# Moving one output matmul from ahead of the second score burst of each batch to behind it, in a fused attention and GEGLU kernel

## The chip, the cores and the metric

The kernel runs on one core of one Trainium2 chip. The metric is device time in microseconds of one execution. A profile of a single execution belongs to each kernel; its span is some 1.8 to 2 us shorter than the metric, as it runs from the first to the last instruction of the program.

## The reference

Eight batches of causal attention (8 heads, 576 positions, 16 "beacon" keys that every query sees, head size 64) are followed by a feed-forward block with a gated GELU on all 4608 rows.

```python
scores = scale * q @ k_all.T            # k_all: beacon keys, then the batch's own
scores = where(causal, -1e9, scores)
a = exp(scores - max);  a /= a.sum()
x = a @ v_all                           # then heads side by side: 4608 x 512
out = (gelu(x @ w_gate) * (x @ w_val)) @ w_out
```

## The kernel before

For each batch b, TensorE carries two jobs in one program order: attention of batch b, and the output product of the feed-forward block of batch b - 1. `o(n)` issues the next n of 48 output matmuls (128x128 by 128x512). `scores(b, ...)` makes one score tile with half-height matmuls (two heads side by side in the array), and lets ScalarE exponentiate it; GpSimd then masks the diagonal. `av_head` and `av` are the products of weights and values, which VectorE normalizes. The output matmuls are there to fill TensorE's time while ScalarE exponentiates.

```python
psum_s = tile_pool(name="psum_s", bufs=3, space=PSUM)    # score tiles
psum_t = tile_pool(name="psum_t", bufs=1, space=PSUM)
psum_o = tile_pool(name="psum_o", bufs=1, space=PSUM)
# ...
def scores(b, *parts):
    s_ps = psum_s.tile([P, 2, 512], FP32, name="s_ps", tag="s")
    # ... matmuls of each part into s_ps
    act(exp_ring[...], s_ps[...], ACT.Exp, scale=QK_SCALE)
    # ... GpSimd's masks
# in the loop over batches, b >= 1; on the right the names that this text uses
# (calls of ahead(2), which issue loads for later batches, are left out)
    o(3)
    scores(b, (0, 0)); scores(b, (0, 2)); scores(b, (0, 1))           # A1 A2 A3
    o(5)
    if b == 1: transpose_pe(1, 3)
    o(5)
    scores(b, (0, 3), (1, 3)); scores(b, (1, 0)); scores(b, (1, 2))   # B1 B2 B3
    o(5)
    av_head(b, 0, 0, psum_t, "t")
    o(1)
    scores(b, (1, 1)); scores(b, (2, 0)); scores(b, (2, 2))           # C1 C2 C3
    av_head(b, 0, 1, psum_t, "t"); turn_dma(b, 0)
    o(7)
    scores(b, (2, 1)); scores(b, (2, 3), (3, 3)); scores(b, (3, 0))   # D1 D2 D3
    av_head(b, 1, 0, psum_o, "o")
    o(5)
    av_head(b, 1, 1, psum_o, "o"); turn_dma(b, 1)
    scores(b, (3, 1)); scores(b, (3, 2))                              # E1 E2
    av(b, 2); turn_dma(b, 2)
    o(6)
    av(b, 3); turn_dma(b, 3)
    o(11)
    # ... then the gate and value matmuls of batch b
```

Score tiles take turns in three buffers (`bufs=3`), so a tile can be written only when the exponential that reads the tile three places before it has ended.

The softmax here doesn't subtract the row's maximum and nothing guards it: scores larger than these inputs give would overflow.

## Time and profile before

| | before |
|---|---|
| time, median of 3 runs | 366.03 us (366.0 to 366.04); the profiled execution took 366.35 us |
| span of the profile | 364.4 us |
| TensorE busy, share of the span | 97% |
| ScalarE, VectorE, GpSimd busy | 52%, 43%, 44% |
| from batch to batch, first score matmul to first score matmul, batches 2 to 7 | 38.877 us (mean of 5) |

The busy share of TensorE can't tell a stream without holes from one with small ones: the matmul records overlap (one lasts 379 ns, but the next starts 216 ns later), so a hole of 100 ns between two starts doesn't show as idle time. One has to compare starts with starts. The last row of the table does that for a whole batch; it repeats within 3 ns.

### The profile page before, as it was taken

To read this page: it belongs to the slowest core of one execution; us is meant where nothing else is said; L and a number is where in the kernel's file an instruction comes from. 1 tells how busy PE (TensorE), PEld (TensorE's weight loads), DVE (VectorE), ACT (ScalarE), POOL (GpSimd) and SP (SyncE) were. 2 spreads that over 40 slices of the span, in tenths; PEclk is the share of its full clock that TensorE was granted. 3 is DMA by queue.
4 is the path that set the end of the run, shared out by engine and by line. 5 is a ranking of instruction groups with operands and counts; after the bars stand their busy time and mean duration, and the time that the engine had idled before them with its cause. 6 is when DMAs were issued, how large, how long until landed. Compare 5 with 4: busy or idle time off the path is not lost.

```text
span 364.4 us, 7627 instructions
## 1 busy us (share of the span) xinstructions
PE 354.3 (97%) x3127; PEld 184.6 (51%) x3170; DVE 155.4 (43%) x305; ACT 189.0 (52%) x243; POOL 161.2 (44%) x288
## 2 busy tenths in 40 slices
PE   7899999999999999999999999999999999999996
PEld 6664446444654456445644464446544564444443
DVE  4546545433454335343533354434444353333332
ACT  3973489136933594339723892379335953321210
POOL 8934388565537452954475554646330530000000
PEclk9999999999999999999999999999999999999999
DMA  7999999799069995999299927991697033000103
GB/s 103 175 203 204 197 124 91 125 187 186 20 121 126 199 87 65 171 216 64 57 146 208 126 35 120 178 197 24 108 142 132 17 64 114 0 0 31 58 34 112
DMA packets 160419, 41.57 MB, mean 114 GB/s; under 512 B 146944, under 2 KB 155904, under 8 KB 160384
## 3 DMA queue, kind: packets, MB, share of 16 engines
q0 software_dynamic: 104848, 19.11, 69.5%
q1 hardware_dynamic: 55536, 21.96, 29.3%
q8 instruction: 25, 0.41, 0.5%
q14 instruction: 10, 0.08, 0.1%
HBM read 38.27 MB, written 9.44 MB: 131 GB/s over the span
## 4 chain that ended last, share of the span: by engine, by line
PE 94%; issue 1%; DMA 1%; DVE 1%; POOL 1%; POOLq 0%; DVEq 0%
PE gv_ps L168 48%; PE o_ps L168 25%; PE x_ps L168 9%; PE s_ps L168 8%; PE v_ps L168 2%; PE g_ps L168 2%; DMA qk<-in_q_dram 1%; PE t_ps L176 1%; DVE qkT L213 1%; POOL qk L111 0%; PE y_ps L176 0%; DVE hT_sb L426 0%; POOL eye L480 0%; DVE o_sb L445 0%; DVE qkT L217 0%
## 5 line engine op out<-in xcount | busy, mean ns | idle before, releaser
L171 ACT ACTIVATE ge_sb<-gv_ps 128x512 bf16<-128x512 f32 x101 | 59.4, 597 | 142.8 <-PE gv_ps L168 140.6
L426 DVE TENSOR_TENSOR hT_sb<-gv_ps,ge_sb 128x512 bf16<-128x512 f32 x101 | 69.0, 691 | 113.5 <-ACT ge_sb L171 111.1
L168 PE MATMUL gv_ps<-xT_sb,wg_sb 128*128 128x512 bf16 x402 | 111.4, 379 | 0.5
L168 PE MATMUL gv_ps<-xT_sb,wv_sb 128*128 128x512 bf16 x388 | 107.9, 379 | 0.4
L171 ACT ACTIVATE expT<-s_ps 128x992 bf16<-128x992 f32 (+3 forms) x112 | 100.6, 974 | 6.5 <-PE s_ps L168 5.4
L168 PE MATMUL o_ps<-wo_sb,hT_sb 128*128 128x512 bf16 (+2 forms) x420 | 99.9, 373 | 2.0 <-issue 0.9
L298 POOL TENSOR_SCALAR_AFFINE_SELECT expT<-expT 128x256 bf16<-128x256 bf16 (+1 forms) x140 | 52.3, 390 | 52.9 <-ACT expT L171 51.8
L168 PEld LDWEIGHTS <-wv_sb 128*128 128x128 bf16 x432 | 42.3, 98 | 50.6
L168 PEld LDWEIGHTS <-wg_sb 128*128 128x128 bf16 x432 | 42.0, 98 | 50.0
L168 PEld LDWEIGHTS <-hT_sb 128*128 128x128 bf16 x444 | 39.9, 98 | 41.7 <-issue 1.7
L168 PEld LDWEIGHTS <-expT 128*128 128x128 bf16 (+1 forms) x960 | 33.6, 97 | 9.8 <-DVE y_sb L334 2.9
L445 DVE COPY o_sb<-o_ps 128x512 f32<-128x512 f32 (+2 forms) x37 | 24.9, 672 | 31.2 <-PE o_ps L168 30.2
L168 PE MATMUL x_ps<-v_sb,expT 128*128 128x65 bf16 (+1 forms) x960 | 37.4, 193 | 0.0
L111 POOL DMA_DIRECT2D v_sb<-in_v_dram x40 | 33.6, 857 | 5.9 <-DMA wv_sb<-in_moe_w_val_dram 1.7
L168 PE MATMUL s_ps<-qkT 64*128 64x80 bf16 (+5 forms) x528 | 33.1, 250 | 2.3 <-DVE qkT L217 1.3
L111 POOL DMA_DIRECT2D k_sb<-in_k_dram x30 | 25.2, 842 | 14.7 <-DMA q_sb<-in_q_dram 11.3
L334 DVE TENSOR_TENSOR y_sb<-x_ps,r_sb 128x320 bf16<-128x320 f32 (+1 forms) x47 | 28.8, 612 | 1.6
L111 POOL DMA_DIRECT2D q_sb<-in_q_dram x30 | 25.3, 874 | 5.2 <-DMA wo_sb<-in_moe_w_out_dram 3.6
L332 DVE RECIPROCAL r_sb<-x_ps 128x5 f32<-128x5 f32 (+1 forms) x47 | 9.6, 204 | 42.3 <-PE x_ps L168 42.3
L168 PEld LDWEIGHTS <-qkT 64*128 64x128 bf16 x528 | 17.1, 95 | 17.8 <-issue 12.9
L377 POOL COPY hold_sb<-xT_sb 128x2 bf16<-128x2 bf16 x6 | 1.1, 186 | 31.1 <-DMA xT_sb<-y_sb 31.1
L111 POOL DMA_DIRECT2D k_sb<-in_beacon_k_dram x6 | 3.2, 534 | 13.4 <-DMA v_sb<-in_v_dram 13.4
(54 smaller groups left out, 123.3 us busy)
## 6 DMA issues: line engine op xcount, KB each, us to landing
out_dram<-o_sb SPq DMA_DIRECT2D x35, 256.0 KB, 7.0
v_sb<-in_v_dram POOLq DMA_DIRECT2D x24, 128.0 KB, 9.1
q_sb<-in_q_dram POOLq DMA_DIRECT2D x18, 128.0 KB, 11.8
k_sb<-in_k_dram POOLq DMA_DIRECT2D x18, 128.0 KB, 5.9
wo_sb<-in_moe_w_out_dram POOLq DMA_DIRECT2D x3, 512.0 KB, 14.4
wg_sb<-in_moe_w_gate_dram POOLq DMA_DIRECT2D x2, 512.0 KB, 11.4
wv_sb<-in_moe_w_val_dram POOLq DMA_DIRECT2D x2, 512.0 KB, 13.0
v_sb<-in_v_dram POOLq DMA_DIRECT2D x8, 112.0 KB, 5.4
```

The lines of the kernel that those rows point to most:

```text
L111: keep(nc.gpsimd.dma_start(out=out_ap, in_=in_ap))
L168: keep(nc.tensor.matmul(out_ap, lhsT, rhs, start=start, stop=stop, **kw))
L171: keep(nc.scalar.activation(out_ap, in_ap, func, **kw))
L176: keep(nc.tensor.transpose(out_ap, in_ap, ident[0:n, 0:n]))
L213: keep(nc.vector.tensor_copy(out_ap, in_ap))
L298: nc.gpsimd.affine_select(out=d, in_=d, pattern=[[0, 2], [1, n]], compare_op=ALU.is_ge, fill=0.0, base=0, channel_multiplier=-1,)
L332: keep(nc.vector.reciprocal(r, x[:, :, :, D:DV]))
L334: nc.vector.tensor_tensor(out=y_of[i][:, :, h0:h1, :].rearrange("p j b d -> p b j d"), in0=x[:, :, :, 0:D], in1=r.to_broadcast([P, h1 - h0 ...
L377: keep(nc.gpsimd.tensor_copy(hold_sb, x[:, 0 : S : S - 1]))
L426: nc.vector.tensor_tensor(out=h_of[ci][:, fi, :], in0=gv_of.pop((ci, fi))[1], in1=ge_sb, op=ALU.mult)
L445: keep(nc.vector.tensor_copy(o_sb[:, ti, c0:c1], o_ps))
```

## The change

The intent: after burst A, ScalarE has nothing to do for 0.21 us. With burst B one output matmul sooner, the exponentials of B should run earlier, and burst C would find its buffer free. The matmul goes to the place between burst B and the first values head instead.

```diff
             ahead(2)
-            o(5)
+            o(4)
             scores(b, (0, 3), (1, 3))
             scores(b, (1, 0))
             scores(b, (1, 2))
             ahead(2)
-            o(5)
+            o(6)
             av_head(b, 0, 0, psum_t, "t")
```

## The prediction

> **What bounds the kernel now.** I read the page first (busy shares and the chain that ended last), then the timeline of batch 4 in narrow windows, then the starts of single matmuls. The page:
>
> ```profile
> PE 354.3 (97%) x3127; PEld 184.6 (51%) x3170; DVE 155.4 (43%) x305; ACT 189.0 (52%) x243; POOL 161.2 (44%) x288
> ...
> PE 94%; issue 1%; DMA 1%; DVE 1%; POOL 1%; POOLq 0%; DVEq 0%
> ```
>
> TensorE is 97% busy and holds 94% of the chain, so the time is TensorE's stream of matmuls plus the holes in it. The first score matmul of each of batches 2 to 7 follows that of the batch before by 40.04 us (batch 2) and then 38.876 us five times, within 2 ns. Batches 2 to 7 thus behave alike, and one can be read for all six.
>
> I name the exponentials of a batch by burst: A1 to A3, B1 to B3 (the burst that moves), C1 to C3, D1 to D3, E1 and E2. Score tiles rotate through three PSUM buffers, so the matmuls of B3 need exponential A3 to have ended, C3 needs B3, D3 needs C3. ScalarE in batch 4:
>
> ```profile
> 165.51 2.75 ACT L171 ACTIVATE expT<-s_ps 128x1024 bf16<-128x1024 f32 x3
> 168.46 5.35 ACT L171 ACTIVATE expT<-s_ps 128x832 bf16<-128x832 f32 x6 [0.21 <-PE s_ps L168]
> 174.00 4.65 ACT L171 ACTIVATE expT<-s_ps 128x992 bf16<-128x992 f32 x5 [0.19 <-PE s_ps L168]
> ```
>
> Burst A is followed by 0.21 us without work, until TensorE brings B1; then B and C run as one block. Starting B earlier fills that hole. Around the C burst (all engines):
>
> ```profile
> 170.13 1.93 ACT L171 ACTIVATE expT<-s_ps 128x928 bf16<-128x928 f32 x2
> ...
> 170.56 0.33 PEld L168 LDWEIGHTS <-qkT 64*128 64x128 bf16 x11 [0.24 <-issue]
> 170.57 0.94 PE L168 MATMUL s_ps<-qkT 64*128 64x80 bf16 x14
> ...
> 171.13 0.11 PEld L168 LDWEIGHTS <-qkT 64*128 64x128 bf16 x3 [0.24 <-issue]
> ```
>
> The weight loads break off and go on at 171.13. That is a hidden wait: B3 ends at 171.079 and C3's first matmul starts at 171.129, 50 ns later. The matmul before it, 512 columns, started at 170.798; such a pair takes 213 ns where nothing waits, and here the gap is 331, so TensorE lost about 115 ns. All of batches 2 to 7 show 115 to 117 ns at this place. It is below what the page counts as idle. This is what the change is after.
>
> The B and D bursts, by contrast, have no break in their weight loads:
>
> ```profile
> 167.25 1.00 ACT L171 ACTIVATE expT<-s_ps 128x992 bf16<-128x992 f32 x1
> ...
> 168.00 0.51 PEld L168 LDWEIGHTS <-qkT 64*128 64x128 bf16 x14 [0.42 <-issue]
> ...
> 168.46 0.86 ACT L171 ACTIVATE expT<-s_ps 128x832 bf16<-128x832 f32 x1 [0.21 <-PE s_ps L168]
> ```
>
> ```profile
> 172.86 0.95 ACT L171 ACTIVATE expT<-s_ps 128x928 bf16<-128x928 f32 x1
> ...
> 173.51 0.48 PEld L168 LDWEIGHTS <-qkT 64*128 64x128 bf16 x18 [0.42 <-issue]
> ```
>
> A3 ends at 168.255 and B3's first matmul starts at 168.414; C3 ends at 173.811 and D3's first matmul starts at 173.920. Taking off the 50 ns of release, the slack is 109 ns at B3 and 59 ns at D3. These two small numbers decide the case.
>
> **What the Trainium skill says.** "TensorE: Matmul & The Clock Gate", Back-to-back issue gap, gives N/2.4 + 2.5 ns between matmuls, 216 ns for 512 columns. The output matmuls here start 215 to 216 ns apart, so it agrees (the 131 ns that the same section gives for a sustained stream does not show). The same page, Part 3, The mechanism, says that matmuls start and end in program order: a score matmul that waits holds back all behind it. The trace agrees, the 115 ns at C3 delays everything after it. "Perfetto Trace Analysis", Tensor Engine Instruction, says that a matmul's end is estimated and only its start is observed; so I work from start to start. The same page, DVE / Act Engine Instruction, puts a semaphore's propagation after the reported end; here that and the start of the matmul together take the 49 to 50 ns above.
>
> **The change part by part.** No instruction is added or removed. On TensorE one 512-column output matmul (216 ns) goes from before burst B to behind it, in each of 7 batches; the other engines keep their order. The number of switches between output matmuls and the half-height score matmuls is the same (each first score matmul comes 312 instead of 216 ns after the output matmul), so the bare stream is unchanged. What moves is the waits. Batch 4, on the old time axis:
>
> - B1 and B2 start 216 ns sooner, their buffers being long free. B1's exponential followed its last score matmul by 298 ns (168.166 to 168.464), so it starts at 168.248. ScalarE is free by then: an exponential of A3's size is followed by the next 0.89 us later in a dense run, at 168.14. B2 and B3 follow densely, so B3 ends at 170.863 instead of 171.079.
> - B3's matmuls would start at 168.414 - 0.216 = 168.198, but A3 frees the buffer only at 168.255 + 0.050 = 168.305. **New wait: 107 ns.** A group that has waited also runs a little raggedly: C3's four matmuls took 308 ns to the next instruction, the same four shapes in B3 294 ns. So the cost is 107 + 14 = 121 ns.
> - The values head and the C burst come 121 ns later. C1's exponential starts 299 ns after its last matmul (170.763 to 171.062), as at B1 and D1, so TensorE sets it, not ScalarE: it moves from 171.062 to 171.183, and C2 and C3, dense behind it, as well.
> - C3's matmuls: ready at about 171.014 + 0.121 = 171.135, buffer free since 170.863 + 0.050 = 170.913. **Wait removed:** 115 + 14 = 129 ns. TensorE is now 8 ns ahead of the old axis.
> - D3's matmuls: ready at 173.920 - 0.008 = 173.912; C3's exponential ends at 173.811 + 0.121 = 173.932, and with 50 ns frees the buffer at 173.982. **New wait: 70 ns**, with 15 ns of raggedness for a 512-column pair (324 against 309 ns, seen in batch 1) 85 ns.
> - Burst E and the last two value heads follow TensorE and move with it. The 54 ns wait before the last value head (on a mask of E2) stays the same.
>
> Sum per batch: 121 - 129 + 85 = **+77 ns**; six batches: +0.46 us.
>
> Batch 1 is different, as a transposition takes a score buffer between A and B:
>
> ```profile
> 51.53 0.16 DVE L200 COPY qkT<-t_ps 128x16 bf16<-128x16 bf16 x1
> ...
> 51.74 0.10 PEld L168 LDWEIGHTS <-qkT 64*128 64x128 bf16 x2 [0.27 <-DVE qkT L200]
> ```
>
> ```profile
> 60.55 0.15 PEld L168 LDWEIGHTS <-expT 128*128 128x128 bf16 x3 [0.16 <-POOL expT L298]
> ```
>
> B3 waits 64 ns for VectorE's copies already, whose time doesn't move, so all 216 ns are lost there. But at 60.55 TensorE waits about 198 ns for GpSimd's masks. GpSimd works densely from the mask behind B3 on; that starts 216 ns sooner, of which about 107 remain after C3's later exponential holds it. So the masks come 0.1 us sooner, TensorE 0.216 us later, and the wait takes up nearly all: +0.02 us. Total: 366.03 + 0.46 + 0.02 = **366.5 us**.
>
> **The rivals.** (1) *The intended gain comes alone.* The C3 wait goes (0.129 x 6 = 0.77 us) and no wait takes its place: 365.3 us. For it: ScalarE's 0.21 us hole is real and just as long as the move. Against it: B3 needs A3, and the 109 ns of slack are less than the 216 ns of the move. Half of this could be true if the release after A3 were quicker than 50 ns, but six batches show 49 to 50 at C3. (2) *One wait for another, nothing else.* If D3 keeps its slack, because C1's exponential is started sooner than 299 ns after its matmuls or C2 and C3 run a little denser, the sum is 121 - 129 = -8 ns per batch: 366.0 us. (3) *The waits pile up.* If batch 1's 216 ns aren't taken up by the mask wait, or the first values head (now 121 ns later) makes the second wait for its buffer (1.51 us between their starts; 1.50 are seen in batch 1, without a wait), it becomes 366.8 us or so. Against it: VectorE's normalization releases the buffer about 70 ns ahead by batch 3's times.
>
> **Range and chances.** The chain above is made of repeating times, and three repeats of the kernel before lie within 0.04 us. The uncertainty is in waits of some tens of ns, times 6 or 7. Between rivals (2) and (3) lie 366.0 to 366.8; half of rival (1) reaches 365.7. So 365.8 to 366.9. A change of 2% is 7.3 us, that is 1 us per batch, about eight times the largest of the waits here: faster 0.01, same 0.98, slower 0.01.
>
> **What would show it.** In the profile after: B1's exponential directly behind A3 instead of 0.21 us after its end; a break in the weight loads of burst B, with B3's first matmul 50 ns behind A3's end; no break in burst C; a hole of about 0.3 us on ScalarE before C1 (B3's end at 170.863, C1 at 171.183) where there was none; a short break in burst D; 38.95 us from batch to batch instead of 38.876. I am wrong if burst B runs without a break (then rival 1), if D has none (rival 2), or if the period of a batch is shorter than before.

## The result

The two kernels were timed together in two sets of rounds. A ratio here is the mean time of one kernel's fast runs over the mean of the other's fast runs in the same rounds, so it isn't quite the ratio of the medians.

| set | after, median (range) | before, median (range) | ratio, 95% interval |
|---|---|---|---|
| first | 366.38 us (365.61 to 367.51), 6 runs | 365.96 us (365.76 to 366.04), 6 runs | 1.0014 (0.9995 to 1.0033) |
| second | 366.39 us (365.93 to 368.44), 6 runs | 365.77 us (365.27 to 366.54), 11 runs | 1.0026 (1.0005 to 1.0047) |

Within 2%, and rather slower than faster. The page of the changed kernel, in the lines that the prediction shows of the kernel before:

```profile
PE 354.1 (97%) x3127; PEld 184.1 (51%) x3170; DVE 155.7 (43%) x305; ACT 189.0 (52%) x243; POOL 161.7 (44%) x288
...
PE 95%; DVE 2%; issue 1%; DMA 1%; ACT 0%; DVEq 0%; POOLq 0%
```

These lines tell nothing of the change. ScalarE's timeline of batch 4 does (start, duration, work, count, idle time before it and what ended it):

```profile
164.69 5.36 ACT L171 ACTIVATE expT<-s_ps 128x1024 bf16<-128x1024 f32 x6
170.37 5.48 ACT L171 ACTIVATE expT<-s_ps 128x992 bf16<-128x992 f32 x6 [0.32 <-PE s_ps L168]
176.08 1.83 ACT L171 ACTIVATE expT<-s_ps 128x992 bf16<-128x992 f32 x2 [0.23 <-PE s_ps L168]
```

A and B are now one block of six: the hole of 0.21 us before B is closed, as intended. But a hole of 0.32 us has opened before C, and it is TensorE that ScalarE waits for there. The timeline of all engines around burst B shows why:

```profile
166.44 1.86 ACT L171 ACTIVATE expT<-s_ps 128x992 bf16<-128x992 f32 x2
...
166.97 0.29 PEld L168 LDWEIGHTS <-qkT 64*128 64x128 bf16 x11 [0.42 <-issue]
...
167.49 0.11 PEld L168 LDWEIGHTS <-qkT 64*128 64x128 bf16 x3 [0.23 <-issue]
```

The 14 weight loads of burst B used to go through in one row; now they break off after 11. The first row holds exponentials A3 and B1; A3 alone ends at 167.439, and B3's first matmul starts at 167.490, 51 ns later. Around burst C:

```profile
169.10 0.95 ACT L171 ACTIVATE expT<-s_ps 128x928 bf16<-128x928 f32 x1
...
169.87 0.55 PEld L168 LDWEIGHTS <-qkT 64*128 64x128 bf16 x14 [0.24 <-issue]
...
170.37 1.00 ACT L171 ACTIVATE expT<-s_ps 128x992 bf16<-128x992 f32 x1 [0.32 <-PE s_ps L168]
```

All 14 loads are in one row: C3's wait is gone. And burst D:

```profile
172.68 0.58 PEld L168 LDWEIGHTS <-qkT 64*128 64x128 bf16 x18 [0.42 <-issue]
```

This took 0.48 us before. D3's wait is too short to break the row up, but the row is 0.10 us longer, and D3's first matmul starts at 173.165, 50 ns after exponential C3 ended at 173.115.

Where the time went, stretch by stretch, from the starts of the first score matmul of each batch (us):

| | before | after | after, second set |
|---|---|---|---|
| start to batch 1 | 47.207 | 46.207 | 46.720 |
| batch 1 to batch 2 | 40.043 | 40.080 | 40.063 |
| batch 2 to batch 7 | 194.383 | 194.752 | 194.750 |
| batch 7 to the end | 82.793 | 82.884 | 82.889 |
| span | 364.426 | 363.923 | 364.422 |

The start-up differs by 1.0 us between profiles, though the programs are the same up to there. From batch 1 on the change costs 0.497 and 0.483 us; the prediction had 0.48. This is why the profiled execution of the changed kernel is shorter than that of the kernel before although the change costs time.

### The profile page after: what moved, and what is told of

Same layout as the page of the kernel before. It is cut to its first block, busy times and chain, and to the rows that moved or that the text cites. A ratio compares the mean times of both kernels' runs of the same rounds, so it can differ in the third digit from the quotient of the medians.

```text
span 363.9 us, 7627 instructions
## 1 busy us (share of the span) xinstructions
PE 354.1 (97%) x3127; PEld 184.1 (51%) x3170; DVE 155.7 (43%) x305; ACT 189.0 (52%) x243; POOL 161.7 (44%) x288
## 4 chain that ended last, share of the span: by engine, by line
PE 95%; DVE 2%; issue 1%; DMA 1%; ACT 0%; DVEq 0%; POOLq 0%
PE gv_ps L168 48%; PE o_ps L168 25%; PE x_ps L168 9%; PE s_ps L168 8%; PE v_ps L168 2%; PE g_ps L168 2%; PE t_ps L176 2%; DVE qkT L213 1%; DMA qk<-in_k_dram 1%; PE y_ps L176 0%; DVE qkT L195 0%; DVE hT_sb L426 0%; DVE qkT L199 0%; ACT qkT L171 0%; DVE o_sb L445 0%
```

## The experiments

The table has one line for each kernel: the time from batch to batch (mean of batches 2 to 7; for three of them without one disturbed batch, see below) and the waits in batch 3, as the gap between the starts of two matmuls, less the gap of the same two where nothing waits (213 ns after a 512-column pair, 32 ns after an 80-column pair).

| kernel | batch to batch, us | wait at B3, ns | at C3 | at D3 |
|---|---|---|---|---|
| before | 38.877 | 0 | 119 | 0 |
| after | 38.950 | 108 | 1 | 70 |
| after, second set (again) | 38.950 | 107 | 1 | 71 |
| two_sooner | 39.166 | 322 | 1 | 71 |
| one_later | 39.094 | 0 | 320 | -1 |
| a3_short | 38.830 | 1 | 1 | 70 |
| after_dlater | 38.990 | 107 | 1 | 0 |
| before_dlater | 39.001 | 0 | 117 | 0 |
| after_d2 | 38.870 | 108 | 1 | 0 |
| half | 38.842 | 0 | 1 | 62 |
| half_dlater | 38.897 | 0 | 2 | 0 |
| before_e | 38.813 | 0 | 121 | 0 |
| b1_only | 38.877 | 0 | 121 | 0 |
| best | 38.706 | 1 | 1 | 0 |

All kernels gave correct results (a3_short too, within tolerance, although half of one tile's weights are stale in it). Where only one execution was timed, its time tells little, as the start-up alone scatters by some 1 us and more (two_sooner 368.06 us, one_later 367.80, a3_short 365.60, after_dlater 367.34, before_dlater 366.31, after_d2 367.81, half 366.02, half_dlater 366.14, before_e 365.21, b1_only 366.28).

### The changed kernel again

No edit. Expected:

> The changed kernel unaltered, timed in five rounds beside the kernel before. My theory (waits of score buffers: 121 ns lost at B3, 129 ns won back at C3, about 83 ns lost at D3) says 38.951 us from batch to batch in every run of it against 38.876 us before, so +0.46 us for six batches and about +0.04 us in batch 1: ratio 1.0013, if the time up to the first score burst of batch 1 is the same. That start-up stretch differed by 1.0 us between the two profiles although its instructions are the same; my theory says that this is run-to-run variation of the first loads, which either kernel can draw. A rival, that the changed kernel itself has a longer or more variable start, expects its start-up to differ from that of the kernel before here too, and its times to spread over more than 1 us again while those of the kernel before stay within 0.3 us.

Measured: ratio 1.0026 (second set above), 38.950 us in each batch, 40.063 us in batch 1. The periods are within 1 ns of the expected ones (the expectation was written after the first profile had shown 38.950 us, so this is a repeat, not a forecast). The times spread by 2.5 us, but those of the kernel before also spread by 1.3 us in these rounds, more than the rival allowed it. The largest time, 368.44 us, belongs to an execution whose granted clock was 0.991 instead of 1.000. Leaving it out is a choice made after the fact; without it the ratio is 366.33 / 365.81 = 1.0014 (the mean of the other five over the mean of the eleven), as in the first set. The start-up, 46.720 us, lies between the two values seen first. In all profiles it lies between 45.98 and 48.79 us; the largest is after_d2's, where the second slice of the granted clock reads 6 tenths:

```profile
PEclk9699999999999999999999999999999999999999
```

So the start-up is a matter of the run, as far as fourteen profiles tell, and not of the change. The record names three chips for the experiments (12, 5 and 10). Periods can be compared across them: batches 2 to 7 of b1_only, which are those of the kernel before, take 38.877 us there as in the first profile.

### Burst B two matmuls sooner

```diff
-            o(4)
+            o(3)
             scores(b, (0, 3), (1, 3)) ...
-            o(6)
+            o(7)
```
(against the changed kernel)

> The second score burst two output matmuls sooner than before (one more than in the change), both behind it. Theory: exponential A3 fixes the release of B3's buffer, so the wait at B3 grows by the whole 216 ns, from 105 to about 321 ns; C3 has no wait; C1's exponential and D3's matmuls move together, so D3's wait stays at 67 ns. From batch to batch 38.951 + 0.215 = 39.166 us. A rival in which ScalarE is fed earlier and the matmuls profit (the intent of the change) expects less than 38.95 us; a rival in which B3's 105 ns come from something of fixed length (a weight load or a switch of modes) expects B3 still at 105 ns and the period unchanged at 38.95 us.

Measured: 39.166 us, exactly as the theory has it. The timeline around burst B in batch 4 now has a wait long enough to be named, and in ScalarE's timeline the hole before C has doubled:

```profile
168.85 0.37 PE L168 MATMUL s_ps<-qkT 64*128 64x384 bf16 x4 [0.16 <-ACT expT L171]
```

```profile
171.94 4.56 ACT L171 ACTIVATE expT<-s_ps 128x992 bf16<-128x992 f32 x5 [0.63 <-PE s_ps L168]
```

The idle time printed, 0.16 us, is what is left of a wait of 322 ns after the modelled end of the matmul before it. Both rivals fall: the 105 ns at B3 aren't of fixed length, and bringing B still sooner gains nothing.

### Burst B one matmul later

```diff
-            o(5)
+            o(6)
             scores(b, (0, 3), (1, 3)) ...
-            o(5)
+            o(4)
```
(against the kernel before)

> The change turned round: the second score burst one output matmul later than in the kernel before (six ahead of it, four behind). Theory: B3 doesn't wait; its exponential ends 216 ns later, so C3 waits 115 + 216 = 331 ns (all 216 ns come on top); C1's exponential is now bound by ScalarE and starts about 0.1 us later; D3 has no wait. From batch to batch 38.876 + 0.216 = 39.092 us. A rival in which the place of this burst doesn't matter as long as ScalarE has work expects 38.88 us.

Measured: 39.094 us. C3 waits 320 ns (331 expected; the stretch from burst B to burst C is 15 ns longer than before, apart from the matmul that left it, so TensorE comes to C3 that much later):

```profile
172.01 0.37 PE L168 MATMUL s_ps<-qkT 64*128 64x384 bf16 x4 [0.16 <-ACT expT L171]
```

B3 and C3 are thus the two ends of one constraint. One matmul sooner, TensorE waits at B3 for A3; one later, it waits at C3 for B3.

### Exponential A3 cut in half

```diff
+        if b > 1 and parts == ((0, 1),):
+            act(exp_ring[:, 0, :, o : o + 248], s_ps[:, :, 0:248], ACT.Exp, scale=QK_SCALE)
+            masks(b, 0, 1)
+            return
         act( ...
```
(against the changed kernel; half of these attention weights stay stale)

> Wrong on purpose. The changed kernel, but from batch 2 on the exponential A3 processes only 248 of its 496 columns for each head (the rest of the attention weights stay stale), so that it frees its score buffer about 0.45 us sooner; nothing else is altered. Theory: the wait at B3 (105 ns) is gone, C3 has none, C1's exponential is back at its old place relative to the output matmuls, so D3 finds TensorE 129 ns earlier and waits about 70 ns + 15. From batch to batch 38.876 - 0.129 + 0.085 = 38.832 us. If B3's break in the changed kernel had another cause than A3's exponential (weight loads, transposes, the moved matmul itself), the break stays and the period stays at 38.95 us.

Measured: 38.830 us. A3 takes 0.59 instead of 1.00 us, and the row of burst B is whole again:

```profile
166.77 0.59 ACT L171 ACTIVATE expT<-s_ps 128x496 bf16<-128x496 f32 x1
...
167.31 0.51 PEld L168 LDWEIGHTS <-qkT 64*128 64x128 bf16 x14 [0.42 <-issue]
```

So it is A3's end that holds B3 in the changed kernel. Without that wait the change would have gained 47 ns per batch; D3's wait, 70 ns, stays and takes the rest.

### Burst D one matmul later, in both kernels

```diff
             turn_dma(b, 0)
-            o(7)
+            o(8)
             scores(b, (2, 1)) ...
             av_head(b, 1, 0, psum_o, "o")
-            o(5)
+            o(4)
```

> The changed kernel, with one output matmul moved from behind the fourth score burst (D) to ahead of it, so that D comes 216 ns later. Theory: D3's new wait (67 ns and 15 ns of raggedness) is gone, as C3's exponential now has 216 - 67 = 149 ns to spare; from batch to batch 38.951 - 0.082 = 38.869 us, which leaves only B3's cost against C3's gain (-8 ns against the kernel before). If the 75 ns that the change cost per batch came from B3 alone, with D's break a mere consequence, the period stays at about 38.95 us.

> The control to that: the same move of an output matmul ahead of the fourth score burst, in the kernel before. There D3 has 59 ns of slack and doesn't wait, so theory says no effect: 38.876 us from batch to batch (C3's wait of 115 ns stays). If a later D burst helps by itself (for example because ScalarE or GpSimd has more time), the period falls below 38.86 us here too.

Measured: 38.990 and 39.001 us. Both expectations failed: it got slower in both kernels, by 40 and by 124 ns. D3's wait did go (last column of the table), but a new one came. In the changed kernel's variant, batch 4:

```profile
176.49 0.39 PEld L168 LDWEIGHTS <-expT 128*128 128x128 bf16 x11 [0.44 <-DVE y_sb L334]
```

The second values head of the pair waits for VectorE, which has still to normalize the first one out of the only `psum_o` buffer. Four output matmuls between the two heads are too few to cover that; five are enough in both kernels. The gap is 328 instead of 216 ns, so the wait is 112 ns, and some 12 ns of ragged starts follow. I had taken the matmul from the wrong place. The sum agrees even so: 38.950 - 0.082 + 0.124 = 38.992.

### Burst D later, with the matmul taken from the end of the batch

```diff
             turn_dma(b, 0)
-            o(7)
+            o(8)
             ...
             turn_dma(b, 3)
-            o(11)
+            o(10)
```
(against the changed kernel)

> Repeat of the test of D3 with the confounder taken away. In the first one the later D burst left only four output matmuls between the two value heads of the second pair, and the second of them waited 112 ns (and 12 of raggedness) for VectorE to empty its buffer. Here, in the changed kernel, the matmul that goes ahead of burst D comes from the eleven at the end of the batch, so five stay between those heads. Theory: no wait at C3, D3 or those heads; from batch to batch 38.951 - 0.082 = 38.869 us. If D3's break isn't worth its length, 38.95 us.

Measured: 38.870 us. Burst D's loads take their old 0.48 us:

```profile
175.28 0.48 PEld L168 LDWEIGHTS <-qkT 64*128 64x128 bf16 x18 [0.42 <-issue]
```

D3's wait with what follows it is thus worth 80 ns, and with it gone the changed kernel is 7 ns per batch faster than the one before: what is lost at B3 and what is won at C3 cancel.

### Half a matmul sooner

The last output matmul of one tile is cut in two of 256 columns, around burst B, and the first matmul of the next tile goes ahead of them.

```diff
-            o(5)
+            o(3)
+            ps_now, ps_next = o_of[b - 1][1], out_ps(1)
+            out_mm(b - 1, 1, 0, ps_next)
+            mm(ps_now[:, 0:256], h_of[b - 1][:, 11, 0:P], wo_sb[:, 11, 0:256], False, False)
             scores(b, (0, 3), (1, 3)) ...
+            out_mm(b - 1, 0, 11, ps_now[:, 256:512], 256, 512)
+            out_store(b - 1, 0, ps_now)
+            o_of[b - 1][1] = ps_next
+            u[0] = 13
             o(5)
```
(against the kernel before)

> The kernel before, with the second score burst only half an output matmul sooner: the last matmul of one output tile is cut in two of 256 columns, one half ahead of the burst, the other behind it. Theory: 108 ns is just the slack that B3 has (109 ns), so B3 waits 0 to 5 ns; B3's exponential ends 108 ns sooner, and C3's wait shrinks from 115 to about 8 ns; D3 then comes 106 to 120 ns sooner while C1's exponential stays, so D3 waits about 50 to 60 ns and 15 ns of raggedness. From batch to batch 38.83 to 38.85 us. If the sum of waits always comes back somewhere (nothing to be gained by the burst's place), 38.88 us.

> Both together: the second burst half an output matmul sooner and the fourth burst one output matmul later than in the kernel before. Theory: no wait of more than some 10 ns is left at B3, C3 and D3; from batch to batch 38.756 to 38.775 us, 0.1 us less than before and 0.18 us less than in the change. If ScalarE is the bound behind it all, the wait turns up at E or at the last values head, and the period stays at 38.83 us or more.

Measured: 38.842 us for the half move, with B3 and C3 both at 0 to 1 ns. Half a matmul is just the slack that B3 had:

```profile
166.53 0.52 PEld L168 LDWEIGHTS <-qkT 64*128 64x128 bf16 x14 [0.32 <-issue]
```

half_dlater made 38.897 us and missed its 38.756 to 38.775; it has the same wait for VectorE as the two kernels above (114 ns in batch 4). That is not ScalarE's bound, the reason that the expectation had named for such a result. Less the 124 ns it would be 38.773.

### The last value heads one matmul later

```diff
             turn_dma(b, 2)
-            o(6)
+            o(7)
             av(b, 3)
             turn_dma(b, 3)
-            o(11)
+            o(10)
```
(against the kernel before)

> The kernel before, with one output matmul moved from behind the last two value heads to ahead of them. They wait 54 ns there for GpSimd's mask of the last exponential, in every batch from 2 on and in both kernels. Theory: that wait goes, with some 5 to 10 ns of raggedness: 38.81 to 38.82 us from batch to batch. A rival: the transposed rows of that last pair are then late for the gate and value matmuls (their transfer landed 0.8 us ahead of its use in batch 4; this takes 0.2 us of it), and the period stays at 38.88 us or scatters.

Measured: 38.813 us. The wait for the mask at the last heads is gone: the largest step between two starts of their matmuls is 39 ns, where it was 84 ns before (an undisturbed one is about 29). In the view the row of their loads shrinks, but it is the starts that measure the wait; first before, then before_e:

```profile
178.85 1.22 PEld L168 LDWEIGHTS <-expT 128*128 128x128 bf16 x30
```

```profile
178.47 0.94 PEld L168 LDWEIGHTS <-expT 128*128 128x128 bf16 x29
```

### The change in batch 1 alone

```diff
-            o(5)
+            o(4 if b == 1 else 5)
             ...
-            o(5)
+            o(6 if b == 1 else 5)
```
(against the kernel before)

> The change in batch 1 alone. Theory: batches 2 to 7 follow each other at 38.876 us as in the kernel before; from the first score matmul of batch 1 to that of batch 2 it takes 40.06 to 40.08 us, as in the two profiles of the changed kernel (40.043 before): B3 waits 280 ns there for VectorE's copies instead of 64, and the 198 ns wait for GpSimd's masks is gone. If the mask wait doesn't take up the loss, it is 40.26 us.

Measured: 40.073 us in batch 1 and 38.877 after it, as expected. In the changed kernel's own profile, B3's loads in batch 1 wait for VectorE's copies (the wait grew from 67 to 283 ns), and the heads that waited for GpSimd's mask run on:

```profile
50.76 0.10 PEld L168 LDWEIGHTS <-qkT 64*128 64x128 bf16 x2 [0.48 <-DVE qkT L200]
```

```profile
59.30 0.69 PEld L168 LDWEIGHTS <-expT 128*128 128x128 bf16 x21 [0.23 <-POOL expT L298]
```

21 loads in one row, where before the row broke off for the mask at 60.55. Nearly the whole 216 ns are taken up by that slack of 198 ns.

### A version meant to beat both

The half move, burst D one matmul later and the last heads one later, both matmuls taken from the end of the batch (`o(8)`, `o(5)`, `o(7)`, `o(9)`).

> A version meant to beat both: the second score burst half an output matmul sooner than in the kernel before, the fourth burst one output matmul later (taken from the end of the batch, so that the value heads keep their five), and the last value heads one output matmul later. Theory: what the half move gave (38.843 us) less D3's wait (57 and 15 ns) less the 54 to 64 ns ahead of the last values: 38.707 to 38.72 us from batch to batch, about 1.0 us less over six batches than the kernel before, ratio about 0.997 and 0.996 against the change. The start-up scatters by about as much from run to run, so the period in the profile tells more than the times. A rival: with two matmuls fewer at the end of the batch the last transposed rows come late for the gate and value matmuls and the gain is lost there.

Measured: 38.706 us in four of five batches, 1 ns below the range that was expected, and 171 ns less than before. The time doesn't show it: 366.13 us (365.39 to 366.42, 6 runs) against 366.04 us (365.04 to 366.56, 11 runs), ratio 1.0001 (0.9987 to 1.0015). In the profiled execution batch 4 took 39.982 us, 1.28 us too long:

```profile
185.56 0.38 PE L168 MATMUL gv_ps<-xT_sb,wg_sb 128*128 128x512 bf16 x1 [1.11 <-DMA xT_sb<-y_sb]
```

TensorE waits for the last transposed rows of the batch. The view of the transfers from 182 to 186 us has that transposition at 4.2 us from issue to landing, where the median of the 28 in that run is 2.6:

```profile
xT_sb<-y_sb SPq DMA_TRANSPOSE x1, 4.2
```

In the records of single transfers, 18 packets of it took up to 1.67 us, while the usual one takes about 0.02. The two other kernels with the half move were held in batch 4 in the same way (by 1.23 and 0.84 us), and their periods above leave that batch out. Groups of such slow packets are also found in other kernels at other times (near 142 and 258 us in several, at 187 us in b1_only), without a delay in the period of their batch.

Another line of the same view says more. In this window the profile counts one transfer of 16 KB as "instruction", by its name the loading of the program; the window from 181 to 186 us of the kernel before has none.

```profile
q8 instruction: 1, 0.02, 2.1%
```

In the records of single transfers of all fourteen profiles, from 44 us on, each of the 40 groups of ten or more slow packets (over 0.8 us each) overlaps such an instruction transfer in time. In batch 4 this transfer starts 17.9 to 18.6 us after the first score matmul in the three kernels with the half move, and 21.8 to 22.7 us after it in the eleven others. In these three it falls on the last transposition of batch 4, so chance is unlikely. That it makes the packets slow isn't shown, as no run moved it alone.

Nor is it shown that the timed executions of this kernel all had such a hold-up, but the sums fit: from batch 1 to the end the profiled execution took 317.38 us against 317.22 us before, and without the 1.28 us it would have been about 1.1 us faster. As it stands I can't call it faster.

## Why the prediction was right

The prediction was right: 366.5 us against a median of 366.38 us, inside its range. That the totals lie so close is partly luck: the start-up alone differs by 1.0 us between the two first profiles, and the rivals' totals of 366.0 and 366.8 us lie inside the range of the timed runs (365.61 to 367.51 us). It is the periods and the waits, not the times, that confirm the mechanism. Its steps, one by one:

- **The stream itself doesn't change.** This agrees with after_d2: with D's wait removed, the period is 7 ns shorter than that of the kernel before, where the prediction's sum for B3 and C3 alone gives 8.
- **B3's new wait, 107 ns and 14 of raggedness, because A3 frees the buffer.** 106 to 108 ns in the two profiles, with the first matmul 51 to 52 ns after A3's end. two_sooner (322 ns, a whole matmul more) and a3_short (wait gone) show A3 to be the cause.
- **C3's wait, 129 ns with raggedness, removed.** It is gone. one_later shows the same wait grow in the other direction. The size was read slightly wrong: the prediction's own 331 - 213 is 118 ns, not 115, and the profile before shows 118 to 120 ns in batches 2 to 7 (by the same count B3's wait in batch 1 is 67 ns, not 64). It matters little, as TensorE comes to D3 sooner by what it gains at C3: 77 ns per batch were predicted and 73 measured.
- **C1's exponential is bound by TensorE and moves with B3's wait.** ScalarE's hole before C, predicted as about 0.3 us, is 0.32 us.
- **D3's new wait, 70 ns and 15 of raggedness.** 70 to 72 ns in the two profiles; 80 ns in all by after_d2. One detail was wrong: the prediction promised a break in the row of D's weight loads, and took its absence as a sign for its second rival. The row only grew by 0.10 us, since the view joins loads less than 150 ns apart; the starts of the matmuls show the wait.
- **Batch 1 loses 0.02 us, as the mask wait takes up the rest.** 0.04 and 0.02 us in the two profiles, and 0.03 in b1_only. The mask wait is gone. GpSimd's mask ended 78 to 97 ns sooner after the batch's first score matmul (13.29 us before; 13.21, 13.20 and 13.21 in the two profiles and b1_only), as predicted, but this wasn't needed: the matmul that had waited for it until 13.35 us now comes at 13.37 to 13.39 us in any case.
- **The sum, 0.48 us.** 0.497 and 0.483 us from batch 1 to the end.

The rival that the intended gain comes alone (365.3 us) falls with B3's wait. The rival of one wait for another, without D3 (366.0 us), is what after_d2 made real by other means. The third, of waits that pile up, didn't occur here, but a wait of its kind (a head's buffer that VectorE hasn't emptied) was met in after_dlater, when I shortened another cover myself.

The one thing that the prediction didn't foresee is the scatter. Three times within 0.04 us looked like a firm base, but the profiled execution of the same kernel had taken 366.35 us, and the start-up can shift by more than the whole effect of the change.

## What to carry to other kernels

A buffer ring with few slots fixes a window for each burst: too late and the next burst waits for this one's reader, too early and this burst waits for the last one's. Before moving work, put a number on the slack at both ends; here 109 ns at B3 and 59 ns at D3 against a move of 216 ns told the outcome to within 0.02 us. Where the step of a schedule is larger than the slack, a smaller step can take part of the gain without that loss (half a matmul won 35 ns per batch and left B3 without a wait, though D3 still waited 62 ns), and any matmul moved must come from a place whose own cover can spare it.

## What the Trainium skill lacked or had wrong

- "Perfetto Trace Analysis", DVE / Act Engine Instruction, says that a semaphore still has to propagate after the reported end, without a number. From the reported end of an exponential to the start of the matmul that waited for it, these runs show 49 to 52 ns in batches 2 to 7, at every burst where TensorE waited by more than 50 ns.
- "TensorEngine Tiling (Array Packing)", Key Properties, says that a change of tiling mode drains TensorE, without a number. From full-height to half-height matmuls the starts are 312 instead of 216 ns apart, and 128 instead of 32 ns on the way back: 96 ns for each switch, which is as much as the waits that this study is about.
- "TensorE: Matmul & The Clock Gate", Back-to-back issue gap, gives 131 ns as a sustained spacing for 512 columns and calls its formula that of an isolated matmul. In the long runs of output matmuls here the starts are 215 to 216 ns apart, as the formula has it.
- No page that I read mentions that single packets of an on-chip transposition can take 1.0 to 2.1 us instead of about 0.02, in groups of 14 to 21, or that such groups come with transfers that the profile counts as "instruction" (40 of 40 groups overlap one here). They held TensorE up by 0.84 to 1.28 us in three profiles.
